# Two issue-order edges around the last routing tile of a top-k attention, gated MLP and routed-MLP kernel

## The chip, the cores and the metric

The kernel runs on one core of one Trainium2 chip. The metric is the device time of one execution in microseconds, the median of several runs; lower is better. Engines are called PE (TensorE), DVE (VectorE), ACT (ScalarE), POOL (GpSimd) and SP (the engine that issues most DMAs); PEld is PE's weight load.

## The reference

Three layers are computed one after the other, for 2 x 576 = 1152 tokens of width 512.

```python
# attention, 8 heads of 64, each query keeps its 32 best scores
scores = scale * np.matmul(q, k.transpose(0, 1, 3, 2))
...
attn = attn / (np.sum(attn, axis=-1, keepdims=True) + 1e-09)
x = np.matmul(attn, v)
# gated MLP with RMS norm, width 1536
...
x = silu * val @ w_out
# routed MLP: 8 experts, each token goes to its best one, capacity 288
expert_idx = np.argmax(x @ w_gate, axis=1)
for i in range(N):
    disp[expert_idx[i], counts[expert_idx[i]]] = x[i]
    ...
h = np.maximum(np.einsum('ecd,edf->ecf', disp, w1), 0.0)
y = np.einsum('ecf,efd->ecd', h, w2)
out[i] = gate_w[i] * y[expert_idx[i], pos[i]]
```

## The kernel before, in words

Tokens are worked in nine tiles of 128 (`NT = 9`). For each tile the attention, the gated MLP (`moe1`) and the routing (`dispatch`) are generators that are traced in interleaved steps. `dispatch(t)` takes the MLP's result `y` of a tile, computes the logits on PE (L504), finds the best expert on DVE (`lg` L507, `m8` L527, `key` L534, `k8` L537, one-hot `oh` L541), counts with two small matmuls how many earlier tokens chose the same expert (L544, L545; L543 counts the earlier tiles alone), turns that into a row number (`scr` L552, `pos` L555, `slot` L565), and scatters the tile's rows into the DRAM buffer `disp` with an indirect DMA on the POOL queue (L567). What is scattered is the row `yd`: `y`, scaled, as two f16 halves, `yh` (ACT, L519) and `yl` (DVE, L520, which reads `yh`), with two numbers for the return. The scale comes from a chain of small DVE instructions (L511 to L517) on the sum of squares of `y` (ACT, L498).

The experts' weights, `w1` and `w2` of eight experts, are 16 matrices of 2 MB, loaded by SP in two halves each (`load`, L721). Number n in the order of loading passes two steps. `size(j, n)` takes sums of squares on ACT (L734, output `junk`), a small matmul on PE (L739) and small DVE steps, and finds a power of two as scale. `convert(j, n)` then splits the weights into an f16 high half and an f16 low half: for n below 4 in four quarters of 1024 columns, two high quarters on ACT (L759), two on DVE (L761), and the four low quarters on DVE (L764). The raw weights lie in buffers that are used again: numbers 2 and 4 share one, numbers 3 and 5 another. So the load of number 5 waits for `convert(3, 3)`.

Expert 0 is worked in two parts: part "a", its first 128 rows, which the earlier tiles have filled, is gathered by a DMA transpose on ACT's queue (L775) before the last tile is scattered; part "b", 48 rows, needs the last tile. Its rows are gathered by an indirect DMA on POOL (`xb`, L830), then transposed by a DMA on SP (`xbT`, L834). `up` (matmuls L847, then `hE` by ACT L857 and DVE L858) and `down` (L847, then `yT` by DVE L866) are the two layers of an expert; `send` transposes the result back on PE (L885) and scatters it to the output by POOL (L889). The order in which they are traced is up a, down a, up b, up 1, down b, and then for each further expert e: up e, down e-1.

What is traced is put in order at compile time: each engine has one static queue, filled by a planner that takes, among what its own model holds ready, what was traced first. On the chip each queue is worked strictly in that order. `tc.issue_after(ins)` adds an edge for that planner: every instruction that the block traces on the engine of `ins` is queued behind `ins`. It is order alone, with no wait on the chip, and instructions of the block on other engines are not touched. The kernel keeps the instructions that such edges point at in `behind[t, name]`: "dve" is the last low half of the gated MLP's hidden values (L421, by way of L437), "pe" the logits' last matmul (L504), "act" the softmax's exponential (L532), "xu" the copy before the logits (L492). The blocks that use them stand at L815 (`convert(2, 2)` behind "dve"), L895 (`up("a", ...)` behind "pe"), L897 (`convert(3, 3)` behind "dve") and L916 (`size(ORDER[4], 4)` behind "act").

Of the kernel before, what the change touches and what calls it, by code (L numbers as in the profile page):

```python
# [14 lines left out]
AF = mybir.ActivationFunctionType  # L15
OP = mybir.AluOpType
# [9 lines left out]
NT = N // P  # L26
# [19 lines left out]
def tile_topk_attention__then__moe__then__moe_routed(  # L46
# [3 lines left out]
    nc = tc.nc  # L50
# [372 lines left out]
    yx, late, behind = {}, [], {}  # L423

    def after(t, engine):

        return tc.issue_after(behind[t, engine].ins)
# [58 lines left out]
    def dispatch(t):  # L486
        y = yx.pop(t)
# [6 lines left out]
        yh, yl = (yd[:, i * DM // 2:(i + 1) * DM // 2].bitcast(F16) for i in range(2))  # L494
        nc.gpsimd.tensor_copy(yd[:, DM + 1:ROW], tok[:, t:t + 1])
        yn = route.tile([P, 8], F32, name="yn")
# [19 lines left out]
            invert(yn[:, 2:3], yn[:, 1:2])  # L516
        nc.vector.tensor_scalar(yn[:, 5:6], yn[:, 1:2], YS, None, op0=OP.mult)  # L517
        if t == NT - 1:
            nc.scalar.activation(yh, y, AF.Copy, scale=yn[:, 5:6])  # L519
            nc.vector.scalar_tensor_tensor(yl, y, yn[:, 5:6], yh, op0=OP.mult, op1=OP.subtract)  # L520
        else:
            nc.scalar.activation(y, y, AF.Copy, scale=yn[:, 5:6])
            nc.scalar.activation(yh, y, AF.Copy)
            nc.gpsimd.tensor_tensor(yl, y, yh, op=OP.subtract)
# [15 lines left out]
        ev = nc.vector if t == NT - 1 else nc.gpsimd  # L540
# [6 lines left out]
        pos = route.tile([P, 4], F32, name="pos")  # L547
# [14 lines left out]
                gather("a", 0, 0, WA, ew, nc.scalar)  # L562
                notes("a", 0, 0, WA, ew, nc.scalar)
        slot = route.tile([P, 1], I32, name="slot")
        ev.tensor_scalar(slot, pos[:, 0:1], pos[:, 1:2], pos[:, 2:3], op0=OP.add, op1=OP.add)  # L565
        nc.gpsimd.tensor_tensor(cum, cum, oh, op=OP.add)
        scat.append(nc.gpsimd.indirect_dma_start(  # L567
            out=disp, out_offset=bass.IndirectOffsetOnAxis(ap=slot[:, :1], axis=0),
# [73 lines left out]
    for p in range(NP):  # L642
        t, hp = divmod(p, 4)
# [12 lines left out]
    for t in range(NT):  # L656
        ew = nc.vector if t in (0, 8) else nc.gpsimd
        t0 = (4 * t + 5) * SL
        at(t0 + 1, ahead(norm(t, ew), 300), 1)
        at(t0 + (12 if t < NT - 1 else 18), ahead(moe1(t, ew), 0), 2.7)  # L660
        at(t0 + 10 + 4 * SL, ahead(dispatch(t), 0), 3 if t < NT - 1 else 1)
    live = []
    slot = 0
# [62 lines left out]
    def size(j, n):  # L726

        e, w = divmod(j, 2)
        raw = raw_of(n)
        sc = ew.tile([P, 13], F32, name="sc", bufs=8)  # L730
        k = 4 if n < 4 else 2
        for g in range(k):
            junk = ew.tile([P, BIG], BF16, name="junk")[:, :2 * BIG // k]
            nc.scalar.activation(junk, raw[:, g * 2 * BIG // k:(g + 1) * 2 * BIG // k], AF.Square, accum_out=sc[:, 9 + g:10 + g])  # L734
        t = sums_of[:, n % 8:n % 8 + 1]
        s16 = ew.tile([P, 4], BF16, name="s16", bufs=2)
        nc.vector.tensor_copy(s16[:, :k], sc[:, 9:9 + k])
        for g in range(k):
            nc.tensor.matmul(t[:, 0:1], ones16, s16[:, g:g + 1], start=(g == 0), stop=(g == k - 1))  # L739
        nc.vector.tensor_scalar(sc[:, 2:3], t[:, 0:1], 1.01, TINY, op0=OP.mult, op1=OP.add)  # L740
        half_bits = sc[:, 3:4].bitcast(I32)
        nc.vector.tensor_scalar(half_bits, sc[:, 2:3].bitcast(I32), 1, 0x7fff0000, op0=OP.logical_shift_right, op1=OP.bitwise_and)
        nc.vector.tensor_scalar(half_bits, half_bits, -1, 0x5f370000 + ((10, 14)[w] << 23), op0=OP.mult, op1=OP.add)
        exponent(sc[:, 7:8], sc[:, 3:4])
        invert(sc[:, 4:5], sc[:, 7:8])
        if w == 0:
            es[e] = sc
        else:
            nc.vector.tensor_tensor(es[e][:, 8:9], es[e][:, 4:5], sc[:, 4:5], op=OP.mult)
        sized[j] = sc  # L750

    def convert(j, n):

        raw, (hi, lo), sc = raw_of(n), place(j), sized.pop(j)
        k = 4 if n < 4 else 2
        for g in range(k):
            r = slice(g * 2 * BIG // k, (g + 1) * 2 * BIG // k)
            if 2 * g < k:
                nc.scalar.activation(hi[:, r], raw[:, r], AF.Copy, scale=sc[:, 7:8])  # L759
            else:  # L760
                nc.vector.tensor_scalar(hi[:, r], raw[:, r], sc[:, 7:8], None, op0=OP.mult)  # L761
        for g in range(k):
            r = slice(g * 2 * BIG // k, (g + 1) * 2 * BIG // k)
            nc.vector.scalar_tensor_tensor(lo[:, r], raw[:, r], sc[:, 7:8], hi[:, r], op0=OP.mult, op1=OP.subtract)  # L764
# [31 lines left out]
    def fetch_w():  # L796
        n = loaded[0]
        loaded[0] += 1
        if n < 2 * E:
            load(ORDER[n], n)  # L800
# [49 lines left out]
    def up(k, e, n):  # L850
        hE[k] = [eb.tile([P, NF2, n], F16, name=f"hE{i}", bufs=2 if n <= W else 1) for i in range(2)]
        for lo, hi in groups(NF2, n):
            a = pacc.tile([P, hi - lo, n], F32, name="acc")
            for c in range(lo, hi):
                product(a[:, c - lo, :], place(2 * e), (xgT[k][:, :KC], xgT[k][:, KC:]), KC, F2, c)
            hh, hl = (x[:, lo:hi, :] for x in hE[k])
            nc.scalar.activation(hh, a, AF.Relu)  # L857
            nc.vector.scalar_tensor_tensor(hl, a, 0.0, hh, op0=OP.max, op1=OP.subtract)  # L858
# [35 lines left out]

    with after(NT - 1, "pe"):  # L895
        up("a", 0, WA)
    with after(NT - 1, "dve"):  # L897
        convert(3, 3)
    last = gather(1, 1, 0, W, eb, nc.sync)
    rest_gather()  # L900
# [8 lines left out]
    def ready():  # L909

        n = done[0]
        done[0] += 1
        if n >= 2 * E:
            return
        if n == 4:
            with after(NT - 1, "act"):  # L916
                size(ORDER[4], 4)
        if n + 1 < 2 * E:
            size(ORDER[n + 1], n + 1)
        convert(ORDER[n], n)  # L920
        fetch_w()

    down("a", 0, WA)
    up("b", 0, WB)
    ready()
    send("a", WA, True)
    up(1, 1, W)
    ready()
    down("b", 0, WB)
    ready()  # L930
    cnt = pback.tile([P, DM], F32, name="back")
    nc.tensor.matmul(cnt[:, :E], ones16, cum, start=True, stop=True)
# [82 lines left out]
```

## Time and profile before

| what | us |
|---|---|
| median of 3 runs (697.99 to 699.74) | 698.01 |
| the profiled execution, its own time | 697.47 |
| its span, first to last instruction | 695.6 |
| PE busy, of the span | 552.8 (79%) |
| DVE busy | 612.3 (88%) |
| ACT busy | 497.0 (71%) |
| POOL busy | 438.2 (63%) |

The profile is of one execution. Times in it count from the span's start; 697.47 - 695.6 = 1.9 us lie outside the span. The busy shares are means over stages with different limits: attention with the gated MLP up to about 545 us, the last tile's routing from there to about 570 us, and the experts' matmuls to about 688 us.

### The profile page before, as it was taken

Reading aid. Unit: us, or ns where it says so; the run is one execution under the profiler, and the core shown is the slowest. Engines: PE = TensorE matmul, PEld = TensorE weight load, DVE = VectorE, ACT = ScalarE, POOL = GpSimd, SP = SyncE. Lnnn points to the kernel's source line nnn. Section 1 sums busy time; section 2 is a strip of 40 time slices with the busy share of each in tenths; the row PEclk is TensorE's granted clock in tenths of the full one; section 3 lists DMA queues with packets and bytes.
Section 4 is the critical chain, followed back from the end, with each engine's and each line's share of the span. In section 5 each row is a group of like instructions: output and inputs, shape, how many; then the busy total and the mean of one; then the engine's idle time right before and its main releaser. Section 6 shows DMA issues by size and latency. Waiting matters only on the chain.

```text
span 695.6 us, 12985 instructions
## 1 busy us (share of the span) xinstructions
PE 552.8 (79%) x4708; PEld 401.2 (58%) x4708; DVE 612.3 (88%) x1215; ACT 497.0 (71%) x959; POOL 438.2 (63%) x521
## 2 busy tenths in 40 slices
PE   1217425467687999999999999999999679999994
PEld 1106314344444666666666666665545469999994
DVE  3999999999999999999999999997158865999960
ACT  3456539569875888878789787887598438988821
POOL 3785889988895987877878779597531110023312
PEclk9999665588989999999999999999999889999998
DMA  8998171475000001000000000000850459999201
GB/s 236 264 327 279 34 243 44 128 228 192 17 1 23 9 31 43 16 32 10 31 8 16 32 9 24 1 2 16 302 197 1 151 125 389 309 328 347 96 21 39
DMA packets 47016, 80.00 MB, mean 115 GB/s; under 512 B 18732, under 2 KB 23340, under 8 KB 46946
## 3 DMA queue, kind: packets, MB, share of 16 engines
q1 hardware_dynamic: 43954, 74.02, 33.5%
q0 software_dynamic: 1792, 4.83, 1.9%
q8 instruction: 39, 0.64, 0.4%
q10 hardware_dynamic: 1200, 0.26, 0.2%
q14 instruction: 31, 0.25, 0.1%
HBM read 64.35 MB, written 12.27 MB: 110 GB/s over the span
## 4 chain that ended last, share of the span: by engine, by line
PE 31%; DVE 24%; issue 14%; POOL 13%; ACT 9%; DMA 7%; SPq 1%; POOLq 0%; ACTq 0%; DVEq 0%
PE pm L450 9%; PE pm L475 6%; DVE r L331 6%; DVE m L334 6%; PE acc L847 4%; POOL pp L351 3%; DVE wbig L155 3%; PE xps L382 3%; DMA wbig<-in_w_out_dram 3%; DVE wbig L157 3%; PE tp L374 2%; POOL out_dram L889 2%; PE tp L308 2%; DVE m L322 2%; DVE wbig L226 2%
## 5 line engine op out<-in xcount | busy, mean ns | idle before, releaser
L450 PE MATMUL pm<-wbig,xn 128*128 128x512 f16 x600 | 154.3, 390 | 6.9 <-ACT xn L420 3.5
L334 DVE MAX8 m<-r 128x8 f32<-128x576 f32 x216 | 156.5, 743 | 0.4
L847 PEld LDWEIGHTS <-split 128*128 128x128 f16 x1728 | 116.7, 100 | 13.7 <-issue 7.2
L308 PE MATMUL tp<-kst,qh 128*128 128x288 f32 (+1 forms) x160 | 64.2, 413 | 65.5 <-ACT s L310 21.4
L351 POOL TENSOR_TENSOR pp<-s,pp 128x576 f32<-128x576 f32 x72 | 102.9, 1442 | 10.1 <-ACT pp L350 9.6
L331 DVE MATCH_REPLACE8 r<-m,r 128x576 f32<-128x576 f32 x144 | 106.1, 738 | 0.0
L450 PEld LDWEIGHTS <-xn 128*128 128x128 f16 x648 | 63.4, 100 | 73.0 <-issue 14.2
L308 PEld LDWEIGHTS tp<-kst,qh 128*128 128x128 f32 (+1 forms) x160 | 32.6, 206 | 92.0 <-ACT s L310 29.0
L475 PE MATMUL pm<-wbig,hT 128*128 128x512 f16 x324 | 77.4, 380 | 7.3 <-DVE wbig L226 4.6
L310 ACT ACTIVATE s<-tp 128x288 f32<-128x288 f32 x144 | 54.7, 410 | 22.3 <-POOL pp L351 18.3
L889 POOL DMA_INDIRECT out_dram<-ob,tos x14 | 22.5, 1609 | 71.6 <-ACT ob L887 56.2
L764 DVE SCALAR_TENSOR_TENSOR split<-raw,sc,split 128x2048 f16<-128x2048 f32 (+1 forms) x32 | 65.8, 2077 | 0.3 <-ACT split L759 0.3
L374 PE MATMUL tp<-ident,pp 128*128 128x128 f32 x324 | 56.7, 294 | 11.0 <-ACT pp L356 10.5
L350 ACT ACTIVATE pp<-s,bias 128x576 f32<-128x576 f32 x72 | 51.9, 772 | 16.0 <-POOL bias L336 15.9
L847 PE MATMUL acc<-hE,split 128*128 128x168 f16 (+2 forms) x864 | 58.8, 228 | 4.0 <-ACT junk L734 1.3
L847 PE MATMUL acc<-xgT,split 128*128 128x168 f16 (+1 forms) x768 | 58.0, 239 | 4.3 <-DMA xgT<-disp 4.3
L734 ACT ACTIVATE junk<-raw 128x2048 bf16<-128x2048 f32 (+1 forms) x32 | 54.1, 1692 | 6.8 <-DMA raw<-in_w_dram 5.7
L356 ACT ACTIVATE pp<-pp,bias 128x576 f32<-128x576 f32 x72 | 56.3, 782 | 3.2 <-POOL pp L351 2.9
L375 ACT ACTIVATE pt<-tp 128x384 f32<-128x384 f32 x108 | 48.8, 492 | 11.7 <-PE tp L374 6.9
L374 PEld LDWEIGHTS tp<-ident,pp 128*128 128x128 f32 x324 | 41.3, 150 | 25.0 <-ACT pp L356 13.8
L382 PE MATMUL xps<-pt,vt 128*64 128x128 f32 (+1 forms) x800 | 55.7, 279 | 0.0
L322 DVE MAX8 m<-s 128x8 f32<-128x576 f32 x72 | 53.6, 745 | 1.8 <-ACT s L310 1.7
(203 smaller groups left out, 1230.4 us busy)
## 6 DMA issues: line engine op xcount, KB each, us to landing
raw<-in_w_dram SPq DMA_DIRECT2D x28, 1024.0 KB, 9.8
wbig<-in_w_out_dram SPq DMA_DIRECT2D x6, 1024.0 KB, 9.0
disp<-wraw SPq DMA_DIRECT2D x18, 257.0 KB, 5.4
qraw<-in_q_l_dram SPq DMA_DIRECT2D x72, 64.0 KB, 2.2
wraw<-in_w_gate_dram SPq DMA_DIRECT2D x8, 512.0 KB, 4.5
split<-in_w_dram SPq DMA_DIRECT2D x4, 1024.0 KB, 7.6
kraw<-in_k_l_dram SPq DMA_DIRECT2D x12, 288.0 KB, 4.1
wbig<-in_w_val_dram SPq DMA_DIRECT2D x3, 1024.0 KB, 8.0
```

The costliest lines, as they stand in the source:

```text
L308: nc.tensor.matmul(sp[:c1], x[:, i, :c1], kst[b, hp][:, i, c * HALF:(c + 1) * HALF], start=(n == 0), stop=(n == 1))
L322: nc.vector.max(m[:, i, 0], s[i])
L331: nc.vector.match_replace(r[i], m[:, i, n - 1], src, -3.0e38)
L334: nc.vector.max(m[:, i, n], r[i])
L351: nc.gpsimd.tensor_tensor(w, s[i], w, op=OP.subtract)
L356: nc.scalar.activation(pp[p][:, i], pp[p][:, i], AF.Exp, bias=bias[:, i, 0:1], scale=0.125, accum_out=sums[t][:, h:h + 1])
L374: nc.tensor.transpose(tp[:, i, :], p2[:, o:o + P], ident)
L382: nc.tensor.matmul(xps[t][rows, hp, c0:c1], v, w, start=(n == 0), stop=(n == 4))
L450: nc.tensor.matmul(a, xn[:, x + c, :], half(i, lo), start=(c == 0 and n == 0), stop=(c == KC - 1 and n == 2))
L475: nc.tensor.matmul(yps, hT[f // KC][:, KC * hi + f % KC, :], half(i, lo), start=(f == 0 and n == 0), stop=(f == NF1 - 1 and n == 2))
L764: nc.vector.scalar_tensor_tensor(lo[:, r], raw[:, r], sc[:, 7:8], hi[:, r], op0=OP.mult, op1=OP.subtract)
L847: nc.tensor.matmul(a, u[:, c, col * P:(col + 1) * P], v[:, c, :a.shape[-1]], start=(c == 0 and n == 0), stop=(c == nk - 1 and n == 2))
```

## The change

`behind` gets two more entries, "slot" (the last tile's slot, a DVE instruction) and "yh" (the high half of its scaled row, an ACT instruction). `convert(3, 3)` is queued behind "slot" in place of "dve": its six DVE instructions, while its two ACT instructions keep their freedom. `size(ORDER[4], 4)` is queued behind "yh" as well as "act": its two passes on ACT. No instruction is added, removed or altered.

```diff
         if t == NT - 1:
-            nc.scalar.activation(yh, y, AF.Copy, scale=yn[:, 5:6])
+            behind[t, "yh"] = nc.scalar.activation(yh, y, AF.Copy, scale=yn[:, 5:6])
...
-        ev.tensor_scalar(slot, pos[:, 0:1], pos[:, 1:2], pos[:, 2:3], op0=OP.add, op1=OP.add)
+        behind[t, "slot"] = ev.tensor_scalar(slot, pos[:, 0:1], pos[:, 1:2], pos[:, 2:3], op0=OP.add, op1=OP.add)
...
-    with after(NT - 1, "dve"):
+    with after(NT - 1, "slot"):
         convert(3, 3)
...
         if n == 4:
-            with after(NT - 1, "act"):
+            with after(NT - 1, "act"), after(NT - 1, "yh"):
                 size(ORDER[4], 4)
```

## Rows read from the trace of the kernel before

**Rows 1.** What PE waited for, 544 to 695.6 us: total, times, longest.

```profile
PE acc L847 <- DMA xgT<-disp: 4.3, 1, 4.3
PE acc L847 <- DMA xbT<-xb: 4.1, 1, 4.1
```

**Rows 2.** DVE in order of time: start, us, line, operation, out<-in, count, [idle before].

```profile
543.70 2.47 DVE L764 SCALAR_TENSOR_TENSOR split<-raw,sc,split 128x1024 f16<-128x1024 f32 x2
546.09 1.40 DVE L761 TENSOR_SCALAR split<-raw,sc 128x1024 f16<-128x1024 f32 x2
547.41 4.86 DVE L764 SCALAR_TENSOR_TENSOR split<-raw,sc,split 128x1024 f16<-128x1024 f32 x4
...
552.26 2.46 DVE L764 SCALAR_TENSOR_TENSOR split<-raw,sc,split 128x1024 f16<-128x1024 f32 x2
554.65 0.15 DVE L507 COPY lg<-px 128x8 f32<-128x8 f32 x1
...
558.00 0.17 DVE L552 SCALAR_TENSOR_TENSOR scr<-px,oh 128x8 f32<-128x8 f32 x1 [1.31 <-PE px L545]
...
558.42 0.26 DVE L565 TENSOR_SCALAR slot<-pos 128x1 int32<-128x1 f32 x1
558.60 0.74 DVE L520 SCALAR_TENSOR_TENSOR yd<-yx,yn,yd 128x512 f16<-128x512 f32 x1
```

**Rows 3.** PE in order of time, the same columns.

```profile
552.09 5.32 PE L847 MATMUL acc<-xgT,split 128*128 128x128 f16 x53 [4.29 <-DMA xgT<-disp]
557.24 0.17 PE L543 MATMUL px<-cum,ones 128*128 128x8 bf16 x1
...
557.77 0.17 PE L544 MATMUL px<-oh,before 128*128 128x8 bf16 x1
...
557.83 2.06 PE L847 MATMUL acc<-xgT,split 128*128 128x128 f16 x34
```

**Rows 4.** ACT in order of time, the same columns.

```profile
555.70 1.89 ACT L734 ACTIVATE junk<-raw 128x2048 bf16<-128x2048 f32 x1
...
557.59 0.71 ACT L519 ACTIVATE yd<-yx,yn 128x512 f16<-128x512 f32 x1
```

**Rows 5.** POOL in order of time: the scatters of the last two tiles.

```profile
541.50 1.12 POOL L567 DMA_INDIRECT disp<-yd,slot  x1 [0.33 <-POOL slot L565]
...
560.12 1.06 POOL L567 DMA_INDIRECT disp<-yd,slot  x1 [1.86 <-DVE hE L858]
```

**Rows 6.** The chain that ended last, in order of time: start, us, what.

```profile
563.27 4.42 DMA xb<-disp,rest
567.71 3.06 DMA xbT<-xb
```

**Rows 7.** Stretches: busy us and instructions of PE, PEld, DVE, ACT, POOL; PE's clock; DMA.

```profile
557.00:566.75 9.75, 8.91 (x152) 8.31 (x149) 7.57 (x18) 6.15 (x8) 2.56 (x3) 1.00 0.29 76
...
570.81:573.60 2.79, 2.79 (x70) 2.79 (x71) 0.00 (x0) 0.00 (x0) 0.00 (x0) 0.50 1.07 286
...
584.24:606.70 22.46, 22.46 (x313) 22.16 (x308) 21.45 (x35) 21.54 (x24) 0.93 (x1) 1.00 1.14 352
```

**Rows 8.** Groups by shape, 559.9 to 600 us: busy us, mean ns, idle before.

```profile
L847 PE MATMUL acc<-hE,split 128*128 128x48 f16 x96 | 2.6, 183 | 0.0
```

**Rows 9.** SP's queue in order of time: the loads of raw weights.

```profile
552.30 0.37 SPq L721 DMA_DIRECT2D raw<-in_w_dram  x1
...
570.51 12.36 SPq L721 DMA_DIRECT2D raw<-in_w_dram  x8
```

**Rows 10.** DMA issues, 540 to 575 us: count, median us to landing.

```profile
xgT<-disp SPq DMA_TRANSPOSE x3, 4.4
...
xgT<-disp ACTq DMA_TRANSPOSE x1, 6.0
```

**Rows 11.** Weights number 5: DVE's last split of it, and its first use on PE.

```profile
587.95 2.34 DVE L764 SCALAR_TENSOR_TENSOR split<-raw,sc,split 128x2048 f16<-128x2048 f32 x1
...
598.69 1.54 PE L847 MATMUL acc<-xgT,split 128*128 128x168 f16 x19
```

## The prediction

> **What bounds the kernel now.** I began with PE's waits from 544 us on, since both edits touch the last tile's routing alone. Two waits stand out, and they are single events [rows 1]: 4.3 us for the gather of part "a" and 4.1 us for `xbT`, the rows of part "b". The first is a transfer from DRAM that neither edit starts earlier. The second ends a chain that the edits do touch. Read backwards: `xbT` takes 3.06 us from 567.71, the indirect gather `xb` 4.42 us from 563.27 [rows 6], the scatter is issued by POOL at 560.12 [rows 5], and before it come `yl` (558.60), `slot` (558.42) and `scr` on DVE, the last of which waited 1.31 us for PE's L545 [rows 2]. After the chain nothing is free: from 584.24 to 606.70 PE is busy all 22.46 us, with DVE and ACT near it [rows 7]. So a start of part "b" that is earlier by x should bring the end forward by x.
>
> In DVE's queue, the logits' copy L507 starts only at 554.65, straight behind a run of splits. After the first two L764 (543.70) come two L761, then four L764, then (behind a single small instruction) two more [rows 2]. The load that needs `convert(2, 2)` finished was issued at 552.30 [rows 9], when the four had just ended; so of the eight L764 the last two, and two of the four, are `convert(3, 3)`, and so are the two L761. In PE's queue, L543 stands behind 53 matmuls of up "a" and L544 behind 62 [rows 3]. L545 follows L544 directly, and for it `scr` waited 1.31 us when DVE had nothing else to do. So two covers lie one above the other: the splits on DVE, and PE's static order beneath them.
>
> **The change part by part.** `convert(3, 3)` off DVE ahead of the slot: 546.09 to 547.41 for the two L761 (1.32 us), half of 547.41 to 552.20 (2.40 us, leaving the last instruction's overlap out) and 552.26 to 554.65 (2.39 us) [rows 2], together 6.1 us. `convert(2, 2)` then ends at about 543.70 + 2.39 + 2.40 = 548.5 and L507 can start there, 6.1 us earlier.
>
> That is not what the slot gains, because PE's queue decides next. The planner put L543 and L544 where it believed their inputs to be ready, and it believed L507 held behind two splits, since it queued it so; without them L507 is 2.39 us earlier in its view. At 2.06 us for 34 matmuls, 61 ns each at the full clock [rows 3], that is 39 matmuls: I expect L544 behind about 62 - 39 = 23 of them. The bounds are 0 and 62. On the chip up "a" starts when its gather lands, and its first 53 matmuls took 5.15 us, 97 ns each [rows 3]; 23 take 2.2 us.
>
> The gather of part "a" may come later. The second half of load 4 is released with `convert(2, 2)`, at 548.5 in place of 552.30 [rows 9], and so runs beside that gather. Transposes without a load beside them took 4.4 us, this one 6.0 with the first half beside it [rows 10]: 1.6 us for a full overlap is the upper bound, nothing the lower; the second half would meet about the last 2.5 of 6 us, so I take 0.6. Then up "a" starts at 552.09 + 0.6 = 552.7, L544 runs at 554.9, `scr` follows 0.2 us later as before (557.77 to 558.00), and from there to the end of `slot` it is as before 558.68 - 558.00 = 0.7 us: slot at 555.8.
>
> `size(4)` off ACT ahead of `yh`: its first pass, 1.89 us from 555.70, stands directly in front of `yh` [rows 4]. Behind the edge `yh` runs when its scale is known, well before the slot, and `yl` (0.74 us) can run while DVE waits for L545. POOL then issues 0.33 us after the slot, as for the tile before [rows 5], in place of 560.12 - 558.68 = 1.4 us after it. The passes of `size(4)` lose 0.7 us of ACT time at most, in a stretch where its load is the later input; I cost them at nothing.
>
> So the scatter goes out at 556.1, 4.0 us earlier, and `xbT` lands at 570.8 - 4.0 = 566.8. PE ends down "a" now at 566.7, then at 567.3 with the late start. The rows are there first, and the 4.06 us gap becomes one of nothing: 4.06 - 0.6 = 3.5 us gained.
>
> The clock adds to it. In the first 2.79 us after the gap PE's granted clock is 0.50, the 1.2 GHz level, for 70 matmuls [rows 7]; 96 of the same shape take 2.6 us in down "b" at full clock, so 70 take 1.9 [rows 8]. Without the gap 0.9 us is saved; if a short gap is left, somewhere between 0 and that.
>
> What is late next: six splits, 6.1 us, now stand behind the slot, among the evictions of part "a" (L858, L866) for which PE waits. PE idles 0.84 us from 557.00 to 566.75 [rows 7], all of which could vanish (the bound below nothing); one eviction that finds two splits ahead of it loses 2.4 us (the bound above). I take a loss of 0.2. On SP, load 5 needs the buffer that `convert(3, 3)` frees. It would free it by about 555.8 + 6.1 + 2 for other DVE work = 563.9, and SP's loads, behind the gathers, come at 570.51 - 4.0 = 566.5 [rows 9]: nothing lost. Even if they were late, number 5 is split by 590.3 and used at 598.69 [rows 11], a cover of 8 us.
>
> Sum: 3.5 + 0.9 - 0.2 = 4.2 us, from the profiled execution's 697.47 (span 695.6 and 1.9 around it) to 693.3. The median of the runs is 0.5 above that execution, so the next median may lie up to 0.5 higher; I name 693.4.
>
> **A rule against it.** The scatter of the tile before was issued while DVE worked through splits and took POOL 1.12 us; the last tile's took 1.06 us [rows 5]. The Trainium skill ("SBUF — State Buffer", section "Who interferes with whom") says that a VectorE instruction in a 2-port mode, or one with two SBUF inputs, holds a port pair that GpSimd needs, for its whole length. By that rule the scatter and the gather `xb`, which would now run among the deferred splits, would each be held. The trace does not bear it out for the issue at 541.50.
>
> **The rivals.** *PE's order stays.* If L544 is still behind some 62 matmuls, the slot moves by the 0.6 us of the late gather, to 559.3, and only `yl` gains: the scatter goes out 0.33 us after the slot, 559.6, half a us earlier. Time 697.0. For it: nothing in the diff touches PE's queue, and the 1.31 us wait of `scr` shows that queue as the last cover. Against it: L543, which needs no one-hot, sits 9 matmuls ahead of L544, so the pair follows DVE's logits. 0.17, with all places between 23 and 62; half of these are faster by over 0.3%.
>
> *POOL's issues are held by the splits.* Each of two indirect DMAs loses up to one L764 (1.2 us, half of 2.39): `xbT` lands at 569.2, a gap of 1.9 us stays, time about 695.3. 0.06, from the pair of 1.12 and 1.06 us.
>
> *The splits block the evictions* (slower). Place: DVE's queue between `slot` and the first L858. If PE's order stays, so that the slot is at 559.3, and all six splits are queued ahead of that eviction, it is 6.1 us late; down "a" ends at 566.7 + 0.6 + 6.1 = 573.4, 2.6 us after the start that part "b" has now, and if PE restarts at the low clock, some 43 matmuls at 97 in place of 61 ns add up to 1.5: 700.1 to 701.6. It decides from about four splits on. For it: splits sat ahead of the logits in just that way. Against it: up "a" was traced ahead of `convert(3, 3)`, so the planner prefers its evictions whenever it holds both ready. 0.11.
>
> *Absorbed later.* DVE is busy 21.45 of 22.46 us after 584.24 [rows 7]; if its deferred work pushes the later splits, the gain is eaten there. Against it stands the 8 us cover. 0.08, within 0.3%.
>
> *Nothing moves* because the planner already ordered it so: rows 2 and 4 show splits ahead of the slot and a pass of squares ahead of `yh`. 0.03.
>
> **How the numbers follow.** The forecast itself has 0.55. Faster by over 0.3% (2.1 us, about what a measurement of this kernel can tell from no change): 0.55 + 0.06 + half of 0.17 = 0.70. Within it: 0.08 + 0.08 + 0.03 = 0.19. Slower: 0.11. The range: best case, no late gather and no stall, 4.06 + 0.9 + 0.84 = 5.8 us gained, 691.7; I put 691.5. At the top, it reaches through the cases of no change to 698.0; the slower rival is left out.
>
> **What would show it.** In the changed profile: L507 at about 548.5 and no split between it and the slot; L544 behind some 23 matmuls of up "a", not 62; `yh` ahead of both `junk` passes; the scatter near 556; no wait of PE on `xbT`, and the clock at 1.00 through part "b". L544 behind 50 or more, a wait on `xbT` over 2 us, or a PE wait on L858 over 2 us would prove the forecast wrong.

## The result and the profile after

The prediction was wrong in sign. The kernel after takes 701.51 us (median of 8 runs, 700.83 to 704.92), the kernel before 698.00 in the same session (8 runs, 694.32 to 699.97): ratio 1.0057, 95% interval 1.0037 to 1.0077. The forecast was 693.4 us, in a range of 691.5 to 698.0.

The profiled run after took 700.98 us with a span of 699.2. What comes ahead of the last tile differs by a few us from execution to execution (the logits' matmul L504 starts at 546.73 before, at 547.52 here, between 543.6 and 549.7 in the experiments). So I compare profiles from the start of L504 on and write +t for t us after it. From there to the span's end the kernel before takes 695.6 - 546.73 = 148.9 us, the one after 699.2 - 547.52 = 151.7.

VectorE after, in order of time (start, us, line, operation, out<-in, count, [idle before]), against [rows 2]:

```profile
544.48 4.86 DVE L764 SCALAR_TENSOR_TENSOR split<-raw,sc,split 128x1024 f16<-128x1024 f32 x4
...
549.32 0.15 DVE L507 COPY lg<-px 128x8 f32<-128x8 f32 x1
...
552.15 0.27 DVE L565 TENSOR_SCALAR slot<-pos 128x1 int32<-128x1 f32 x1
552.33 1.40 DVE L761 TENSOR_SCALAR split<-raw,sc 128x1024 f16<-128x1024 f32 x2
...
564.19 0.15 DVE L874 CAST to<-xb 48x1 int32<-48x1 f32 x1 [4.94 <-DMA xb<-disp,rest]
...
565.36 0.68 DVE L858 SCALAR_TENSOR_TENSOR hE<-acc,hE 128x512 f16<-128x512 f32 x1
```

The edit does what it says. No split of weights 3 stands ahead of the logits, and `slot` is at +4.6 where it was at 558.42 - 546.73 = +11.7. The line of `xb` is new: a cast of part "b"'s row numbers waits 4.94 us for the gather, with the second eviction of up "a" (565.36) behind it in the queue. POOL after, against [rows 5]:

```profile
542.29 1.12 POOL L567 DMA_INDIRECT disp<-yd,slot  x1 [0.34 <-POOL slot L565]
...
553.83 3.22 POOL L567 DMA_INDIRECT disp<-yd,slot  x1 [2.88 <-ACT junk L734]
559.10 0.97 POOL L830 DMA_INDIRECT xb<-disp,rest  x1 [2.04 <-DMA disp<-yd,slot]
```

The scatter starts at +6.3 instead of +13.4, but takes 3.22 us instead of 1.06. PE after, in order of time, against [rows 3] and [rows 6]:

```profile
549.53 0.19 PE L543 MATMUL px<-cum,ones 128*128 128x8 bf16 x1 [0.95 <-DVE lg L507]
550.47 0.17 PE L544 MATMUL px<-oh,before 128*128 128x8 bf16 x1 [0.74 <-DVE pos L549]
...
552.85 6.78 PE L847 MATMUL acc<-xgT,split 128*128 128x128 f16 x96 [2.19 <-DMA xgT<-disp]
...
566.10 6.25 PE L847 MATMUL acc<-hE,split 128*128 128x128 f16 x83 [5.57 <-DVE sc L137]
572.18 2.59 PE L847 MATMUL acc<-xbT,split 128*128 128x48 f16 x96
...
582.05 2.58 PE L847 MATMUL acc<-hE,split 128*128 128x48 f16 x96
584.48 0.17 PE L932 MATMUL back<-cum,ones 128*128 128x8 bf16 x1
586.95 1.75 PE L847 MATMUL acc<-xgT,split 128*128 128x168 f16 x22 [2.30 <-DMA raw<-in_w_dram]
...
590.85 0.19 PE L739 MATMUL st<-s,ones 128*128 128x1 bf16 x2 [0.43 <-DVE sc L740]
...
598.20 2.19 PE L847 MATMUL acc<-hE,split 128*128 128x168 f16 x28 [3.00 <-DVE sc L743]
```

L543 and L544 now stand ahead of all matmuls of up "a", and the wait on `xbT` is gone; its matmuls run at full clock. But 5.57 us of waiting stand in down "a", ahead of part "b". The releaser named there, L137, is only the small VectorE instruction that ended next; what came late is the eviction at 565.36, behind the cast. PE's low clock has moved there with the gap. Before, down "a" and part "b" were

```profile
561.96 4.79 PE L847 MATMUL acc<-hE,split 128*128 128x128 f16 x83 [0.55 <-DVE sc L742]
570.81 3.69 PE L847 MATMUL acc<-xbT,split 128*128 128x48 f16 x96 [4.05 <-DMA xbT<-xb]
```

and after, a window in down "a" (columns as in [rows 7]) shows a granted clock of 0.70:

```profile
566.75:570.81 4.06, 4.06 (x55) 4.06 (x53) 4.02 (x3) 1.39 (x1) 0.00 (x0) 0.70 1.03 174
```

The 83 matmuls take 6.25 us for 4.79, and part "b" starts at 572.18 - 547.52 = +24.7, no earlier than before (570.81 - 546.73 = +24.1). Then come 2.30, 0.43 and 3.00 us between 584 and 598, where before PE was busy for all of 22.46 us [rows 7]. After down "b" PE issues the count L932 at 584.48 - 547.52 = +37.0; before, up 2's first matmul followed it at 584.24 - 546.73 = +37.5 [rows 7]. So of the 4.2 us forecast, 0.5 had arrived there, and the next 14 us lost 5.7. Over the whole stretch from up "a" to PE's last matmul, PE idles 12.7 us for 9.1 before and is busy 124.9 us for 125.9.

The waits of 2.30 and 3.00 us are for evictions that stand behind the next load's work; the releasers named in their lines, a load and L743, only ended close by. ScalarE after:

```profile
573.26 1.91 ACT L734 ACTIVATE junk<-raw 128x2048 bf16<-128x2048 f32 x1 [5.12 <-DMA raw<-in_w_dram]
...
580.01 1.91 ACT L734 ACTIVATE junk<-raw 128x2048 bf16<-128x2048 f32 x1 [1.11 <-DMA raw<-in_w_dram]
...
581.92 1.99 ACT L759 ACTIVATE split<-raw,sc 128x2048 f16<-128x2048 f32 x1
583.82 0.57 ACT L857 ACTIVATE hE<-acc 128x504 f16<-128x504 f32 x1
```

and VectorE:

```profile
580.38 1.28 DVE L761 TENSOR_SCALAR split<-raw,sc 128x2048 f16<-128x2048 f32 x1
581.69 4.62 DVE L764 SCALAR_TENSOR_TENSOR split<-raw,sc,split 128x2048 f16<-128x2048 f32 x2
586.23 0.67 DVE L858 SCALAR_TENSOR_TENSOR hE<-acc,hE 128x504 f16<-128x504 f32 x1
...
592.80 2.34 DVE L764 SCALAR_TENSOR_TENSOR split<-raw,sc,split 128x2048 f16<-128x2048 f32 x1
...
597.38 0.67 DVE L858 SCALAR_TENSOR_TENSOR hE<-acc,hE 128x504 f16<-128x504 f32 x1
```

The second eviction of up 1 has its ScalarE half behind a pass of squares of load 6 and the high split of load 5 (583.82), its VectorE half behind all three splits of load 5. It ends at 586.23 + 0.67 = 586.90, and PE, which needs its accumulator, goes on at 586.95. In the same way up 2's first eviction (597.38) stands behind load 6's splits, and PE goes on at 598.20. In the kernel before, all three VectorE evictions of up 1 are queued ahead of load 5's splits:

```profile
579.23 0.68 DVE L858 SCALAR_TENSOR_TENSOR hE<-acc,hE 128x504 f16<-128x504 f32 x1 [3.61 <-ACT hE L857]
...
582.26 0.68 DVE L858 SCALAR_TENSOR_TENSOR hE<-acc,hE 128x504 f16<-128x504 f32 x1 [0.31 <-ACT hE L857]
...
582.93 0.50 DVE L858 SCALAR_TENSOR_TENSOR hE<-acc,hE 128x336 f16<-128x336 f32 x1
...
583.97 1.28 DVE L761 TENSOR_SCALAR split<-raw,sc 128x2048 f16<-128x2048 f32 x1
```

The sums' matmul L739 of load 5 is there in down "b" after 34 matmuls; after, it is in up 1 after 59. An edge on the last tile has made the planner lay out the queues differently 30 us further on, though no line of the diff names these instructions.

### The profile page after: what moved, and what is told of

Its sections match the earlier page's. It is cut to its first block, busy times and chain, and to the rows that moved or that the text cites. A ratio compares the mean times of both kernels' runs of the same rounds, so it can differ in the third digit from the quotient of the medians.

```text
span 699.2 us, 12983 instructions
## 1 busy us (share of the span) xinstructions
PE 555.2 (79%) x4708; PEld 401.8 (57%) x4708; DVE 611.9 (88%) x1215; ACT 496.9 (71%) x959; POOL 441.6 (63%) x521
## 4 chain that ended last, share of the span: by engine, by line
DVE 29%; PE 25%; issue 14%; POOL 14%; ACT 9%; DMA 6%; SPq 1%; POOLq 0%; ACTq 0%; DVEq 0%
PE pm L450 9%; DVE r L331 6%; DVE m L334 6%; PE pm L475 5%; DVE wbig L155 4%; PE xps L382 3%; POOL pp L351 3%; DVE wbig L157 3%; DVE m L322 3%; POOL out_dram L889 2%; DMA raw<-in_w_dram 2%; PE tp L308 2%; ACT junk L734 2%; PE tp L374 2%; DVE wbig L226 2%
## 5 line engine op out<-in xcount | busy, mean ns | idle before, releaser
L889 POOL DMA_INDIRECT out_dram<-ob,tos x14 | 23.8, 1701 | 68.4 <-ACT ob L887 53.5
L764 DVE SCALAR_TENSOR_TENSOR split<-raw,sc,split 128x2048 f16<-128x2048 f32 (+1 forms) x32 | 65.7, 2079 | 1.4 <-ACT split L759 1.4
L375 ACT ACTIVATE pt<-tp 128x384 f32<-128x384 f32 x108 | 48.7, 492 | 11.7 <-PE tp L374 6.8
```

## The experiments

Each group is timed beside the kernel before on one chip: e1 to e4 (before: median 697.88), e5 to e8 (698.36), e9 to e11 (698.52), e12 (699.02). The ratios are those on record, with their 95% intervals; they are not the quotients of the medians. The diffs are against the kernel after (that of e8 against the kernel before), with the handles they name added to `behind`. The letters in the quoted texts are theories: H, the cast that waits for `xb` ahead of an eviction; E, evictions behind splits; P, the scatter slowed beside splits; L, load 5 and what hangs on it; R, the planner's new order for loads 5 and 6; A and B are defined where they come up; S means the squares of load 4 in e1 to e4, and a bound further back in e6.

The diff without its second edit gives the same queues on every engine, instruction for instruction, so the second edit adds nothing to the first.

**e1, the second edit alone:** `convert(3, 3)` back behind "dve".

```diff
-    with after(NT - 1, "slot"):
+    with after(NT - 1, "dve"):
         convert(3, 3)
```

> Only the second edit: the squares of weights 4 behind the scaled row on ScalarE, the split of weights 3 where it was. Theory H (head of line): the changed kernel is slow because the early slot lets the planner queue a cast that waits for the gather of part b ahead of the second hE eviction on DVE; without the first edit that order does not arise, DVE's splits still stand ahead of the logits, and the time is that of the kernel before, 698 within 0.3%. Rival S (squares): the scatter of the last tile started in the changed trace just as the first pass of squares ended (553.8), so it is the moved squares that hold it; then this kernel alone shows a late scatter and 1 to 3 us more than before.

Measured 699.42 us, ratio 1.0005 (0.9984 to 1.0027): no change. With the queues just compared, the loss belongs to the deferred splits.

**e2, the change with the casts of part b and expert 1 late:** they (L874, L878) are queued behind the last `yT` of part "a".

```diff
+            with after("a", "yT") if (k, apart) in (("b", True), (1, False)) else ExitStack():
                 to = target(k, i, m, apart)
```

> The changed kernel, with the three small casts of the output rows (part b and expert 1) queued behind the eviction of down a; no other instruction changes its place. Theory H: PE's wait of 5.6 us in down a falls below 1 us, down a ends 4 to 5 us earlier, and the time falls from 701.5 to 696.5 to 698. Rival E (evictions behind splits): what costs the time is the 2.3 and 3.0 us for which PE waits later, between 584 and 599 us, for evictions queued behind splits of weights 5 and 6; then the earlier end of down a is lost there again and the time stays above 700.

Measured 702.89 us, ratio 1.0061 (1.0033 to 1.0089). What PE waited for from 545 us on, as in [rows 1] (total, times, longest):

```profile
PE st L739 <- DVE s L737: 3.9, 1, 3.9
PE acc L847 <- DVE sc L743: 2.6, 1, 2.6
...
PE acc L847 <- DMA xbT<-xb: 1.2, 1, 1.2
PE acc L847 <- DVE sc L137: 0.5, 1, 0.5
```

The wait in down "a" falls from 5.6 to 0.5 us, and nothing is won: 3.9 us have gone to the sums' matmul of load 5 in up 1, whose data are not there yet. H names a wait that is really there, but not what sets the time.

**e3, the splits behind the last eviction of up "a"** instead of behind the slot, and **e4**, the same with the casts late.

```diff
-    with after(NT - 1, "slot"):
+    with after("a", "hE"):
         convert(3, 3)
```

> The changed kernel, but the split of weights 3 behind the last hE eviction of up a in place of the slot; the casts stay ahead of that eviction. DVE has then nothing to do while POOL issues the last scatter. Theory P (port): the scatter took POOL 3.2 us in place of 1.1 because DVE worked through splits beside it; here it takes 1.0 to 1.3 us and lands 2.9 us after its start, the gather of part b lands 2 to 3 us earlier, and PE's wait in down a falls from 5.6 to about 3 us. Rival L (load): the second half of weights 4, which is still in flight then, stretches it; then it takes 3 us here too.

> Both: casts behind the eviction of down a, split of weights 3 behind the last hE eviction of up a. Theories H and P together: no wait of PE over 1 us from the start of up a to the end of up b, the low clock after the gap gone, part b starting about 4 us earlier than in the kernel before, and a time of 693.5 to 696. Rival E: evictions queued behind later splits take it back, and the time is 697 or more.

Measured 707.17 us, ratio 1.0117 (1.0084 to 1.0149), and 708.26, ratio 1.0136 (1.0109 to 1.0162). The scatter of e3, with VectorE idle beside it, and load 5's first pass of squares:

```profile
552.73 1.06 POOL L567 DMA_INDIRECT disp<-yd,slot  x1 [3.40 <-DVE to L874]
```

```profile
583.05 1.91 ACT L734 ACTIVATE junk<-raw 128x2048 bf16<-128x2048 f32 x1 [3.08 <-DMA raw<-in_w_dram]
```

So P holds (1.06 in place of 3.22 us), and a fast scatter does not save the time. `convert(3, 3)` frees load 5's buffer; done later, it lets load 5's first squares start at 583.05 - 545.89 = +37.2 (before 576.72 - 546.73 = +30.0), and e3 is 9.3 us slower than before. Load 5 has no cover of 8 us. Not all of the 9.3 us is waiting: from up "a" on, PE in e3 is busy 131.6 us at a mean granted clock of 0.92, before 125.9 us at 0.95.

**e5 to e8, loads 5 and 6 held where the kernel before has load 5:** PE's sums behind the last matmul of up 1 (up 2), VectorE's splits behind their last eviction. e5 and e7 have the late casts of e2 as well; e8 is the hold on the kernel before. e7 holds load 5 alone (`HELD = {5: 1}`) and leaves out the last two parts of the diff, which trace load 6's turn behind up 2.

```diff
+    HELD = {5: 1, 6: 2}
     def ready():
...
+        if n in HELD:
+            with after(HELD[n], "mm"):
+                size(ORDER[n], n)
-        if n + 1 < 2 * E:
+        if n + 1 < 2 * E and n + 1 not in HELD:
             size(ORDER[n + 1], n + 1)
-        convert(ORDER[n], n)
+        with after(HELD[n], "hE") if n in HELD else ExitStack():
+            convert(ORDER[n], n)
...
     down("b", 0, WB)
-    ready()
...
         up(e, e, W)
+        if e == 2:
+            ready()
```

> The change with the casts of part b late (as e2), and with loads 5 and 6 held: their sums on TensorE are queued behind the last matmul of up 1 (up 2), their splits on VectorE behind the last eviction of up 1 (up 2), as the order of the kernel before had it for load 5. Theory R (the planner's new order for loads 5 and 6 eats the gain): the wait of L739 in up 1 (3.9 us in e2), the 2.3 us before the second eviction of up 1 and the 2.6 to 3.0 us in up 2 go; the stretch from the last logits matmul L504 to the end is 145 to 148 us (before 148.9, after 151.7, e2 152.4), the median 694 to 697. Theory L (load 5 and what hangs on it bounds, wherever it is queued): a wait of the same size shows up at the moved L739 or in down b, the stretch stays at 151 to 153, the median 700 to 703. Theory P (the slow scatter): xbT alone decides; the stretch is 149 to 150, the median 698 to 699.

> The change with loads 5 and 6 held as in e5, but with the casts of part b where the change has them, ahead of the second eviction of up a. Theory R alone: the 5.6 us wait in down a stays and nothing takes it up later, so the median is 3 to 5.6 us above that of e5, 698 to 701, stretch 149 to 152. Theory S (something behind still takes up slack: the casts' wait is hidden by a later bound): within 1.5 us of e5. Theory L: as the change itself, 701.5.

> As e5, but only load 5 is held; load 6 stays where the planner puts it. Theory R: the waits of up 1 go, those of up 2 (2.6 to 3.0 us, an eviction behind the splits of load 6) stay or come back in part: the median is between e5 and e2, 1.5 to 3 us above e5. If the two are the same, load 5 was the whole of it. Theory L: no better than e2, 702.9.

> The kernel before with loads 5 and 6 held in the same way. Its own order has load 5 there already, so theory R expects no change: 697 to 699, stretch 148 to 150. If it is faster by as much as e5 is against the change, the hold is worth something by itself and e5's gain says nothing on why the change failed.

Measured: e5 698.20 us, ratio 1.0000 (0.9979 to 1.0020); e6 698.10, 0.9997 (0.9977 to 1.0017); e7 698.40, 1.0001 (0.9974 to 1.0027); e8 698.85, 1.0003 (0.9980 to 1.0026). The hold takes back the whole loss, as R has it, but not to R's 694 to 697, and gives none of the forecast gain. e7 is no slower than e5, so by its text load 5 is the whole of it. e5's 698.20 lies where its text put P, that `xbT` alone decides. But casts early or late make 0.1 us, as S has it, though e6 still waits in down "a" and starts part "b" at 569.12 - 543.62 = +25.5, e5 at 564.24 - 544.20 = +20.0; so neither `xbT` nor the start of part "b" decides:

```profile
PE acc L847 <- DVE sc L137: 4.6, 1, 4.6
```

```profile
564.24 2.60 PE L847 MATMUL acc<-xbT,split 128*128 128x48 f16 x96 [0.74 <-DMA xbT<-xb]
```

```profile
569.12 2.58 PE L847 MATMUL acc<-xbT,split 128*128 128x48 f16 x96
```

(e6's wait, then part "b" in e5 and in e6.)

**e9 and e10, ScalarE held too:** squares of load 5 (6) behind the first ScalarE eviction of up 1 (up 2); e9 on e5, e10 on e6.

```diff
-            with after(HELD[n], "mm"):
+            with after(HELD[n], "mm"), after(HELD[n], "hh"):
```

> As e5, with ScalarE's squares of load 5 (6) queued as well behind the first ScalarE eviction of up 1 (up 2). In e5 the evictions of part b and of up 1 still stand on ScalarE behind squares that wait for load 5. Theory A (it is these that eat the gain of e5): the waits of 1.2, 1.4 and 1.3 us between 29 and 45 us after L504 go, the stretch from L504 to the end falls from 150.0 to 146 to 147.5, the median to 694 to 696. Theory B (the chain of loads and splits bounds the end; TensorE only waits somewhere else): the stretch stays at 149 to 151, the median at 697.5 to 699, and the waits come back later, past 85 us after L504.

> As e9, with the casts of part b early, as the change has them. Theory A: the 4.6 us wait in down a now has nothing behind it that would take it up, so the median is 3 to 4.6 us above e9. Theory B: within 1.5 us of e9.

Measured 700.18 us, ratio 1.0007 (0.9987 to 1.0026), and 701.02, 1.0041 (1.0021 to 1.0061). The early waits shrink as A wants, but the time does not; in e9 3.7 us come back at +75 and 2.5 at +112. That is nearer to B than to A, but B is not met: it put the waits past +85, and e9's stretch (152.8) and median lie above its ranges too. e10 is within 1.5 us of e9, as B wants.

**e11, one edge alone on the change:** squares of load 5 behind part "b"'s ScalarE eviction; **e12** adds the late casts.

```diff
+            behind[k, "hh"] = nc.scalar.activation(hh, a, AF.Relu)
...
-            size(ORDER[n + 1], n + 1)
+            with after("b", "hh") if n == 4 else ExitStack():
+                size(ORDER[n + 1], n + 1)
```

> The change with one more edge alone: ScalarE's squares of load 5 are queued behind part b's ScalarE eviction. Theory A: the 2.3 us wait in up 2's start goes, 699 to 700. Theory R (the sums and splits of loads 5 and 6 ahead of the evictions on TensorE and VectorE, which this edge moves only through the planner): 700 to 702, unless the planner happens to place them later, and then as low as e6, 698.

> e11 with the casts of part b late, as in e2. In e11 one long wait is left after the last tile, 4.6 us in down a, behind the casts that wait for xb. If PE's start of part b sets the end, as the prediction had it, the wait goes and nothing takes it up: 690.5 to 693, stretch 142 to 144. If load 5 (its sums matmul stands in up 1) and the chain of splits behind it set the end, the wait comes back at that matmul or soon after, and the time stays within 1.5 us of e11: 694 to 697, with a wait of 2 to 4 us at L739 in up 1.

Measured 695.50 us, ratio 0.9945 (0.9922 to 0.9967), and 695.01, ratio 0.9954 (0.9928 to 0.9980): both faster than both kernels, by more than either text for e11 allowed. PE's waits in e11:

```profile
PE acc L847 <- DVE sc L137: 4.6, 1, 4.6
PE acc L847 <- DMA xgT<-disp: 2.1, 1, 2.1
...
PE acc L847 <- DVE s L737: 0.9, 1, 0.9
```

and VectorE in e11, where the planner now lays up 1's evictions between the splits of load 5:

```profile
582.08 1.28 DVE L761 TENSOR_SCALAR split<-raw,sc 128x2048 f16<-128x2048 f32 x1
...
583.35 0.67 DVE L858 SCALAR_TENSOR_TENSOR hE<-acc,hE 128x504 f16<-128x504 f32 x1
583.94 2.34 DVE L764 SCALAR_TENSOR_TENSOR split<-raw,sc,split 128x2048 f16<-128x2048 f32 x1
```

The waits of 2.3 and 3.0 us are gone, and up 2 runs without a gap. In e12 the wait of 4.6 us goes as well and comes back as 2.9 us at the sums of load 5, with the same time: the second outcome of its text.

```profile
PE st L739 <- DVE s L737: 2.9, 1, 2.9
```

In the kernel before this edge alters no queue: part "b"'s eviction stands ahead of these squares there anyway. So the gain of e11 against before needs the change. How much of it is the change itself and how much the queues behind it, which in e11 differ from those of before too, is not shown: the layout of e11 was not tried on the kernel before. Nor is it separated which of the moves that the planner made after this one edge counts (ScalarE's, the interleaved splits, the sums' matmul after 83 matmuls of up 1 instead of 59).

**One table for all.** The stretch from L504 to the end in three terms: until the first split of load 5 on VectorE (L761) starts, from there to the end of the last L764, from there to the end, each rounded by itself. Each row is one execution: differences of a us or two in it need not be the kernel's. In e1, for example, 96 matmuls near the end took 8.77 us at a granted clock of 0.80, which take 7.12 before.

| kernel | first split of load 5 | block of splits | rest | sum |
|---|---|---|---|---|
| before | 37.2 | 86.0 | 25.6 | 148.9 |
| after | 32.9 | 86.2 | 32.6 | 151.7 |
| e1 | 39.0 | 84.7 | 27.3 | 151.0 |
| e2 | 33.7 | 86.3 | 32.4 | 152.4 |
| e3 | 43.7 | 87.3 | 28.3 | 159.4 |
| e4 | 45.8 | 87.6 | 27.4 | 160.9 |
| e5 | 37.5 | 84.9 | 27.6 | 150.0 |
| e6 | 38.1 | 85.2 | 27.6 | 150.9 |
| e7 | 37.8 | 84.6 | 27.6 | 150.0 |
| e8 | 38.9 | 84.6 | 25.7 | 149.3 |
| e9 | 34.6 | 92.0 | 26.2 | 152.8 |
| e10 | 38.0 | 89.6 | 26.1 | 153.8 |
| e11 | 35.7 | 85.2 | 25.6 | 146.5 |
| e12 | 33.5 | 87.6 | 25.6 | 146.8 |

The block in before, after and e11, as windows (columns as in [rows 7], the third busy time being VectorE's):

```profile
583.97:669.97 86.00, 82.06 (x1130) 80.99 (x1127) 82.54 (x131) 71.83 (x77) 17.68 (x9) 1.00 0.81 253
```

```profile
580.38:666.60 86.22, 79.29 (x1142) 78.21 (x1140) 82.19 (x131) 72.13 (x77) 19.97 (x9) 1.00 0.76 255
```

```profile
582.08:667.35 85.27, 84.31 (x1216) 83.77 (x1214) 83.04 (x133) 71.49 (x78) 18.79 (x9) 1.00 0.78 246
```

VectorE is busy 95 to 97% of the block in all three, and but for e9 and e10 the block takes 84.6 to 87.6 us whatever the last tile does. I read VectorE as the bound from load 5 on. This is argued, not shown: no run took work off VectorE, and PE is nearly as full, or fuller (82.1 of 86.0 us before, 84.3 of 85.3 in e11). Before, PE idles 3.9 us in the block, and the end follows 25.6 us behind it. After, the block ends 4.1 us earlier (119.1 for 123.2), but PE idles 6.9 of its 86.2 us, is 7.0 us behind at its end (32.6 for 25.6), and the sum is 2.8 us worse. In e11 the block ends 2.3 us earlier, PE idles 1.0 us in it, and the rest is 25.6 again. The hold of e5 to e7 puts the first split of load 5 back to where it was before (37.5 to 38.1), which would explain why it wins nothing. An earlier first split is not enough by itself, either: e12's comes 2.2 us ahead of e11's, but VectorE then idles 4.6 us in the block, 2.2 in e11, and both blocks end at +121.

## Why the prediction was wrong, step by step

**Right: the edit's own path.** L507 starts at +1.8 instead of +7.9, 6.1 us earlier as worked out. `xbT`'s matmuls find their rows there, the wait of [rows 1] is gone, and they run at full clock: 96 take 2.59 us, 3.69 before. `yh` runs ahead of both passes of squares. Four terms on the way were off and nearly cancelled, by luck:

- L544 stands behind no matmul of up "a", not behind some 23, so `slot` came 7.1 us earlier, not 2.9. The planner moved the whole pair, not by the 2.39 us that I credited it with.
- The gather of part "a" is not later: up "a" starts at +5.4 before and at +5.3 after.
- POOL issues 1.4 us after the slot (552.42 to 553.83), not 0.33. The slot is not what it waits for last. The scatter writes `disp`, and its queue entry also waits for the gather of part "a", which reads `disp`; that gather is what up "a" waits for, too. In the eleven kernels with an early slot the scatter starts 0.97 to 1.15 us after up "a"'s first matmul (after: 553.83 - 552.85 = 0.98), while its distance from the slot's end varies from 1.35 to 1.93. The prediction had no such term. By it a still earlier slot would not start the scatter earlier.
- The scatter takes 3.22 us, not 1.06.

The gather `xb` starts at 559.10 - 547.52 = +11.6, before at 563.27 - 546.73 = +16.5: 4.9 us earlier for 4.0 forecast. None of this reached part "b", which starts 0.6 us later than before.

**Wrong: "I take a loss of 0.2".** The step "What is late next" failed. It looked for splits ahead of part "a"'s evictions and set its upper bound at one eviction behind two of them, 2.4 us. Measured: 5.57 us for an eviction behind a cast that waits for `xb`, then 2.30 and 3.00 us for evictions of up 1 and up 2 behind splits of loads 5 and 6. I had treated the queues as fixed but for the two moved blocks; the planner laid out all of them anew. That this order is the loss is shown by the holds: e6, which has the change's early casts, is at 0.9997 of before, the change at 1.0057. The 5.57 us, the longest of the three, is not what costs the time: e6 still waits 4.6 us there, and the order of load 5 alone (e7) takes the loss back. Nor was the 0.9 us of the clock saved: part "b" gains 1.1 us (2.59 for 3.69), and down "a", behind its own gap, loses 1.5 (6.25 for 4.79). The rival "The splits block the evictions" gave 700.1 to 701.6, and 701.5 was measured, but its place, between the slot and the first L858, is not where it happened: up "a" runs its 96 matmuls without a gap. The match of the number is luck.

**Wrong: "a start of part "b" that is earlier by x should bring the end forward by x".** In e12 part "b" starts at 563.59 - 543.65 = +19.9, 4.1 us earlier than before (570.81, +24.1), and the end comes 2.1 us earlier (146.8 for 148.9). In e11 it starts 1.6 us later than before (572.15 - 546.41 = +25.7), and the end comes 2.4 us earlier. e12 against e11 and e5 against e6 move this start by 5.8 and 5.5 us and the medians by 0.5 and 0.1:

```profile
572.15 2.58 PE L847 MATMUL acc<-xbT,split 128*128 128x48 f16 x96
```

```profile
563.59 2.60 PE L847 MATMUL acc<-xbT,split 128*128 128x48 f16 x96 [0.60 <-DMA xbT<-xb]
```

(Part "b" in e11 and in e12.) I read the end as tied to the work from load 5 on. I had read VectorE's 21.45 of 22.46 us [rows 7] and priced it as the rival "Absorbed later", 0.08; of the rivals it comes nearest.

**Wrong: "a cover of 8 us" for load 5.** It was taken from when its weights are used, but the work behind load 5 has no such slack: e3 made its squares 7.2 us late and lost 9.3 us. The gain that the change does hold comes by way of SP, which issues the loads behind the gathers, at 567.00 - 547.52 = +19.5 in place of +23.8 [rows 9]:

```profile
567.00 12.27 SPq L721 DMA_DIRECT2D raw<-in_w_dram  x8
```

That starts the block 4.4 us earlier. After gives it all back on PE; e11 keeps 1.6 us of the early start, its block is 0.8 us shorter, and the sum is 2.4 us better than before.

**Wrong: "The trace does not bear it out".** The row set against the Trainium skill's rule tested nothing. In the kernel before, VectorE was idle or in a short L421 for most of the scatter from 541.50 to 542.62:

```profile
541.53 0.69 DVE L421 TENSOR_TENSOR hT<-pm,hT 128x512 f16<-128x512 f32 x1 [1.07 <-ACT hT L420]
542.14 1.64 DVE L761 TENSOR_SCALAR split<-raw,sc 128x1024 f16<-128x1024 f32 x2
```

Only its last half us met a split. The rival built on the rule allowed 1.2 us for each indirect DMA; the scatter lost 2.2 us and the gather's issue nothing (0.97 us, with VectorE idle).

**Open.** Each profile is one execution; e2's is its fastest (698.24 of a median of 702.89), as are those of e5, e10 and e12, and those of e4 and e9 are their slowest. Which engine or load bounds the stretch from load 5 on, why e2's runs spread so far (698.24 to 707.59), why the block of splits is longer in e9 and e10, and which of the planner's moves e11 owes its time to, was not traced further.

## What to carry to other kernels

When queues are filled by a planner, an edge on a few instructions is a new layout of everything behind them: compare the order of every queue well past the edit, and look for evictions that have come to stand behind work whose data arrive late. Before crediting a closed gap to the end, find the engines that are nearly full behind it and ask whether their work can start earlier or wait less: here 5.5 us in the start of part "b" changed the time by 0.1 us. A change that loses can be one edge short of a gain: here 701.5 us became 695.5.

## Not expected of the hardware

An indirect DMA on POOL takes three times as long beside splits on VectorE: the same 128-row scatter takes 3.22 us after, 3.01 in e2 and 3.30 in e11, with splits running, and 1.06 us before and in e3 and e4, with VectorE all but idle beside it. In e3 and e4, as after, the second half of load 4 was still to come (its squares wait until 554.63 in e3), so the load is not what holds the scatter. The Trainium skill ("SBUF — State Buffer", section "Who interferes with whom") says that a VectorE instruction with two inputs in SBUF contends with a GpSimd instruction that reads SBUF; by that rule L764, which reads the raw weights and the high half, would hold the scatter up, and these runs agree.
